# Order of the pieces within each visit to the halved array in an attention and feed-forward kernel

## The chip, the cores and the metric

The kernel runs on one core of a Trainium2 chip. The metric is the device time of one execution in microseconds. Three runs of the kernel before gave 1127.61, 1128.57 and 1129.76 us; the median is 1128.57 us.

## The reference

Two layers read the same input and a gate mixes them. The one is attention over four segments of 512 rows, with 32 heads of 20 columns; each segment also reads a memory that the earlier segments wrote. The other is a gated feed-forward layer, 640 wide with 1728 hidden columns. Cut to what matters here:

```python
for s in range(N):                       # N = 4 segments, L = 512 rows, 32 heads, Dh = 20
    logits = einsum("bhqd,bhkd->bhqk", qs, ks) * scale + mask
    p = softmax(logits, axis=-1)
    a_dot = einsum("bhqk,bhkd->bhqd", p, vs)
    a_mem = num / den                    # read of the memory of the earlier segments
    o = g * a_mem + (1.0 - g) * a_dot
    M = M + einsum("bhld,bhle->bhde", pk, vs)
...
b = (silu(x @ w1) * (x @ w3)) @ w2
return sigmoid(x . gate_w) * (o @ wo) + (1 - sigmoid(x . gate_w)) * b
```

The mask takes -1e9 for keys with an index above that of the query, so of the four blocks of 128 keys a block of 128 queries needs only those up to its own: 128, 256, 384 or 512 keys.

## The kernel before, in words

TensorE works on the projections and the feed-forward layer with the whole array (the shape `128*128` in the profile): 15 matmuls of 512 columns into one bank for a block of q, k, g or u (line 261), or a chain of matmuls of 320 columns for v (L372), f (L523) and op (L765). Between them stands the attention, whose contraction is only 60 or 62 rows. Two heads are laid one above the other, head 0 at partitions 0 and up, head 1 at 64 and up, and each head's matmul uses one half of the array's rows (`60*128` and `62*128`). Here a stretch of such matmuls is called a visit to the halved array, and the two matmuls of the two heads a piece.

For each pair of heads there are two kinds of unit:

- `s_unit(p, x)`, lines 560 to 580: the logits with queries in the partitions, from which VectorE takes each row's maximum (line 578, tile `m`). `x` = 0 holds the query blocks 0 and 1, pieces of 128 and 256 columns in one bank for each head; `x` = 1 a piece of 384; `x` = 2 a piece of 512.
- `t_unit(p, x)`, lines 596 to 613: the logits again, turned, with the row maxima as two more rows of the contraction (62 in place of 60), which ScalarE takes through exp into the tile `P` (line 609) and GpSimd masks (line 612). `x` = 0 is a piece of 512, `x` = 1 one of 384, `x` = 2 holds key blocks 3 and 2, pieces of 128 and 256 columns.

So a unit holds two banks, one for each head, and a unit with `x` = 0 of s or `x` = 2 of t holds two pieces in each. The banks come from `bank_tile` (line 120), which hands out eight in turn and takes the oldest free one; a bank is given again when the reader of its former tile is done.

Two pairs of heads make a quad (32 quads). `attention()` (line 712) runs through 40 slots for a quad; at slots 5, 15, 25 and 35 stands a visit, and in slot 5 `pv_quad` (line 617, tile `o`) comes ahead of it, on an array cut into four column strips (`128*32`). In each quad `m`, s units of quad `m` and t units of quad `m - 1` are issued; the table `VISITS` (line 709) says which: `(i, x)` is the pair of the quad and the unit. Between the visits a main loop hands out matmuls of the projections and the feed-forward layer by a credit in time. TensorE's order is that of the program; the order of the other engines is chosen by a scheduler when the kernel is built.

After the s units of a quad, `max_rows` (line 582) splits and turns the maxima and DMAs on GpSimd's queue put them into the two extra rows of `qk` (`qk<-mr`, line 594), for which the t units wait.

Of the kernel before, what the change touches and what calls it, by code (L numbers as in the profile page):

```python
# [17 lines left out]
P = 128  # L18
# [19 lines left out]
def gated_mix(ctx: ExitStack, tc: tile.TileContext, xT, wqk, wv, w13, w2, w2h, wo, beta, out):  # L38
# [81 lines left out]
    def bank_tile(name, hold=None):  # L120


        k = free.pop(0)
        ps = pp.tile([P, L], F32, tag=f"b{k}", name=name, bufs=1)
        if hold:
            held[k] = -hold
        else:
            free.append(k)
        return ps
# [410 lines left out]
    def load_pair(p):  # L540

        j = 2 * p
        c, h = divmod(j, H)
        t = qk[p % NST]
        for mb in {DH * h // P, (DH * h + 2 * DH - 1) // P}:
            assert ("q", c, mb) in stored and ("k", c, mb) in stored
        assert ("v", c, 3) in stored
        for i in range(2):
            here(nc.gpsimd.dma_start(t[64 * i:64 * i + RH], qkd[c][RH * (h + i):RH * (h + i + 1)]))  # L549
        if h % 8 == 0:  # L550
            bank["v"] = v = vg[j // 8 % NVG]
            here(nc.sync.dma_start(v[:, :, :VG], vd[c][:, :, VE * h:VE * h + VG]))
        if p % 2 == 0:
            bank["m"] = sp.tile([P, 16], F32, tag="m", name=f"m{j}", bufs=2)
        for i in range(2):
            o = VE * (h % 8 + i)
            heads[j + i] = dict(c=c, h=h + i, v=bank["v"][:, :, o:o + 32])
        pairs[p] = dict(t=t, m=bank["m"])

    def s_unit(p, t):  # L560

        u = pairs[p]
        m = u["m"]
        ps = [bank_tile(f"s{p}_{t}_{i}") for i in range(2)]
        for qb in ((0, 1), (2,), (3,))[t]:
            n = P * (qb + 1)
            o = 256 if qb == 1 else 0
            for i in range(2):
                q, k = (u["t"][64 * i:64 * i + RH, w] for w in range(2))
                nc.tensor.matmul(ps[i][:, o:o + n], q[:, qb * P:(qb + 1) * P], k[:, :n],  # L570
                                 start=qb != 1, stop=qb != 0, skip_group_check=True)
        for i in range(2):
            for qb in ((0, 1), (2,), (3,))[t]:
                n = P * (qb + 1)
                o = 256 if qb == 1 else 0
                junk = sp.tile([P, L], BF, tag="junk", name="junk", bufs=1)
                a = 8 * (p % 2) + 4 * i + qb
                nc.vector.tensor_tensor_reduce(out=junk[:, :n], in0=ps[i][:, o:o + n], in1=mask[:, L - n:],  # L578
                                               scale=1.0, scalar=-3.0e38, op0=ALU.add, op1=ALU.max,
                                               accum_out=m[:, a:a + 1])  # L580
# [15 lines left out]
    def t_unit(p, t):  # L596

        u = pairs[p]
        if t == 0:
            u["P"] = sp.tile([P, 2, 1280], F32, tag="P32", name=f"P{p}", bufs=NP)  # L600
        ps = [bank_tile(f"t{p}_{t}_{i}") for i in range(2)]
        for kb, q0, o in (((0, 0, 0),), ((1, P, 0),), ((3, 384, P), (2, 256, 256)))[t]:
            for i in range(2):
                q, k = (u["t"][64 * i:64 * i + RH + 2, w] for w in range(2))
                nc.tensor.matmul(ps[i][:, o:o + L - q0], k[:, kb * P:(kb + 1) * P], q[:, q0:],  # L605
                                 start=kb != 2, stop=kb != 3, skip_group_check=True)
        o, b, n = ((0, 0, 512), (512, 0, 384), (896, P, 384))[t]
        for i in range(2):
            last["exp"] = nc.scalar.activation(u["P"][:, i, o:o + n], ps[i][:, b:b + n], AF.Exp, scale=SCALE)  # L609
        for a, n in (((0, 1),), (), ((512, 1), (896, 2)))[t]:  # L610
            d = u["P"][:, :, a:a + n * P].rearrange("p h (a b) -> p h a b", b=P)
            nc.gpsimd.affine_select(d, d, pattern=[[0, 2], [0, n], [1, P]], base=0, channel_multiplier=-1,  # L612
                                    compare_op=ALU.is_ge, fill=0.0)
# [3 lines left out]
    def pv_quad(p):  # L617

        ps = bank_tile(f"o{p}")
        for kb, (o, n) in enumerate(PSEG):  # L620
            for i in range(4):
                nc.tensor.matmul(ps[32 * i:32 * i + 32, kb * P:], heads[2 * p + i]["v"][:, kb],  # L622
                                 pairs[p + i // 2]["P"][:, i % 2, o:o + n],
                                 start=kb == 0, stop=kb == 3, skip_group_check=True)
        ot = sp.tile([P, L], F32, tag="oq", name=f"oq{p}", bufs=1)
        nc.scalar.copy(ot, ps)
        c, h = heads[2 * p]["c"], heads[2 * p]["h"]
        nc.scalar.dma_start(od[c][h:h + 4].rearrange("h e n -> (h e) n"), ot)
        q = p // 2 % 8
        for b in OUT.get(q, ()):  # L630
            after(8, o_load, c, b)
        if q == 7:
            after(6 if c < NSEG - 1 else 2, o_sums, c)
# [63 lines left out]
    def after(n, f, *a):  # L697
        soon.append([n, f, a])

    def tick():  # L700
        for e in list(soon):
            e[0] -= 1
            if e[0] <= 0:
                soon.remove(e)
                e[1](*e[2])

    NQUAD = NJ // 4

    VISITS = {5: (((0, 0), (0, 1)), ((0, 0),)), 15: (((0, 2), (1, 0)), ((0, 1),)),
              25: (((1, 1), (1, 2)), ((0, 2),)), 35: ((), ((1, 0), (1, 1), (1, 2)))}  # L710

    def attention():


        for m in range(-1, NQUAD + 2):
            for n in range(40):
                if m == -1 and n < 40 - LEAD:
                    continue
                if n in VISITS:
                    us, ut = VISITS[n]  # L720
                    yield "visit"
                    if n == 5 and 0 <= m - 2 < NQUAD:
                        pv_quad(2 * m - 4)
                    if 0 <= m < NQUAD:
                        for i, x in us:
                            s_unit(2 * m + i, x)
                    if 0 <= m - 1 < NQUAD:
                        for i, x in ut:
                            t_unit(2 * m - 2 + i, x)
                    if n == 25 and 0 <= m < NQUAD:  # L730
                        after(6, max_rows, 2 * m)
                elif n in ((22, 32) if m < 0 else (27, 37)) and m + 1 < NQUAD:
                    load_pair(2 * (m + 1) + (n > 27))
                tick()
                yield m
# [160 lines left out]
    for n, (_, g) in enumerate(head):  # L896
# [7 lines left out]
        elif n == 9:  # L904
            gates()
    stores(True)
    att = attention()

    def begin():
# [101 lines left out]
```

## Time and profile before

| | |
|---|---|
| median of the three runs | 1128.57 us |
| profiled execution | 1128.27 us |
| its span in the profile | 1126.6 us (1.67 us lie around it) |
| PE, matmuls | 1118.2 us busy, 99% of the span |
| DVE, ACT, POOL | 51%, 43%, 48% busy |
| granted TensorE clock | 0.999 |

PE is TensorE's matmuls, PEld its weight loads, DVE VectorE, ACT ScalarE, POOL GpSimd, SP the queue of SyncE. In a timeline row stand the start in us, the length in us, the engine, the line, the operation, the tile written and the tiles read, the shape of the array, the operand's size and the count; rows of one kind that follow each other are merged, and the length of a merged row runs from its first start to its last end. A matmul's end in the profile is modelled and overlaps the next one, so the argument goes by starts. A window that ends between two instructions shows the start of each.

### The profile page before, as it was taken

The page shows a single profiled execution, that of the slowest core. Times are in us where ns is not written, and L with a number is a line of the kernel's source. Part 1 is how long each engine was busy: PE and PEld are TensorE (multiplying, and loading weights), DVE is VectorE, ACT ScalarE, POOL GpSimd, SP SyncE. Part 2 cuts the span into 40 slices and gives each one's busy share as a digit, 9 for nine tenths or more (in the row PEclk, how much of TensorE's full clock was granted, in tenths as well). Part 3 has the DMA queues.
Part 4 walks back from the last instruction along what each step waited for, and adds up shares of the span by engine and source line. Part 5 has one row for each costly group of instructions (what it writes and reads, how often), then busy time and mean ns, then how long its engine had stood idle before and what let it go on. Part 6 is the DMA issues. An engine that isn't in the chain of part 4 may idle for free.

```text
span 1126.6 us, 19474 instructions
## 1 busy us (share of the span) xinstructions
PE 1118.2 (99%) x6953; PEld 902.7 (80%) x6953; DVE 572.2 (51%) x1718; ACT 483.6 (43%) x988; POOL 544.2 (48%) x731
## 2 busy tenths in 40 slices
PE   9999999999999999999999999999999999999998
PEld 6988777877877888888977776788768778877888
DVE  5032564345555553565243667774546665651544
ACT  6255244544343242255355644535543444344040
POOL 5053356455455453454255346645764555465140
PEclk9999999999999999999999999999999999999999
DMA  9265753334243324535377874455654333342122
GB/s 328 80 235 204 235 135 94 96 81 114 79 112 103 97 65 121 140 86 177 109 244 246 269 213 133 103 133 167 165 130 106 86 100 95 100 136 76 49 59 94
DMA packets 85809, 152.01 MB, mean 135 GB/s; under 512 B 19920, under 2 KB 32720, under 8 KB 85712
## 3 DMA queue, kind: packets, MB, share of 16 engines
q1 hardware_dynamic: 55920, 95.01, 26.8%
q0 software_dynamic: 22880, 41.86, 15.5%
q10 hardware_dynamic: 6912, 13.90, 3.3%
q8 instruction: 55, 0.90, 0.3%
q14 instruction: 42, 0.34, 0.1%
HBM read 95.25 MB, written 54.53 MB: 133 GB/s over the span
## 4 chain that ended last, share of the span: by engine, by line
PE 93%; issue 2%; DVE 2%; DMA 1%; POOL 1%; ACT 0%; SPq 0%; POOLq 0%; DVEq 0%
PE g L261 17%; PE f L523 17%; PE u L261 16%; PE v L372 6%; PE k L261 6%; PE q L261 6%; PE o L622 6%; PE s L570 5%; PE op L765 4%; PE t L605 4%; PE pm L426 1%; PE nd L339 1%; DVE junk L578 1%; DMA qk<-mr 1%; PE pkt L411 1%
## 5 line engine op out<-in xcount | busy, mean ns | idle before, releaser
L578 DVE CUSTOM_DVE_ANT_0 junk<-s,mask 128x128 bf16<-128x128 f32 (+3 forms) x512 | 251.1, 490 | 190.5 <-PE s L570 151.3
L116 POOL TENSOR_TENSOR W<-wr,W 128x640 fp32r<-128x640 f32 (+1 forms) x126 | 197.6, 1572 | 204.2 <-ACT W L115 161.5
L609 ACT ACTIVATE P<-t 128x384 f32<-128x384 f32 (+1 forms) x384 | 174.5, 533 | 163.6 <-PE t L605 160.8
L261 PE MATMUL g<-X,W 128*128 128x512 f32 x840 | 216.3, 401 | 0.0
L612 POOL TENSOR_SCALAR_AFFINE_SELECT P<-P 128x256 f32<-128x256 f32 (+1 forms) x192 | 94.2, 497 | 235.0 <-ACT P L609 233.6
L523 PE MATMUL f<-W,ht 128*128 128x320 f32 x1312 | 204.7, 313 | 0.7 <-ACT acc L529 0.5
L261 PE MATMUL u<-X,W 128*128 128x512 f32 x780 | 201.0, 401 | 0.0
L523 PEld LDWEIGHTS f<-W,ht 128*128 128x128 f32 x1312 | 194.6, 189 | 7.2 <-issue 3.2
L261 PEld LDWEIGHTS g<-X,W 128*128 128x128 f32 x840 | 153.6, 188 | 39.8 <-issue 5.7
L261 PEld LDWEIGHTS u<-X,W 128*128 128x128 f32 x780 | 143.1, 188 | 36.2 <-issue 3.9
L115 ACT CAST W<-wr 128x640 fp32r<-128x640 f32 (+1 forms) x133 | 95.5, 730 | 74.7 <-PE u L261 23.1
L594 POOL DMA_DIRECT2D qk<-mr x128 | 73.5, 576 | 49.0 <-DVE mr L589 40.0
L531 DVE SCALAR_TENSOR_TENSOR acc<-f,cgate,acc 128x320 f32<-128x320 f32 x128 | 69.4, 547 | 40.4 <-PE f L523 39.7
L116 POOL TENSOR_TENSOR ht<-ft,ht 128x512 fp32r<-128x512 f32 x52 | 67.2, 1292 | 46.1 <-ACT ht L115 45.9
L261 PE MATMUL k<-X,W 128*128 128x512 f32 x300 | 77.1, 403 | 0.0
L261 PE MATMUL q<-X,W 128*128 128x512 f32 x300 | 75.4, 402 | 0.7 <-DVE X L116 0.6
L622 PE MATMUL o<-P,vg 128*32 128x512 f32 (+3 forms) x1024 | 75.7, 436 | 0.0
L765 PE MATMUL op<-W,oT 128*128 128x320 f32 x480 | 75.3, 313 | 0.0
L765 PEld LDWEIGHTS op<-W,oT 128*128 128x128 f32 x480 | 71.2, 189 | 2.5 <-issue 1.6
L372 PE MATMUL v<-W,X 128*128 128x320 f32 (+1 forms) x480 | 72.1, 311 | 0.5 <-DVE m L578 0.5
L372 PEld LDWEIGHTS v<-W,X 128*128 128x128 f32 x480 | 71.0, 189 | 1.4 <-DVE m L578 0.9
L549 POOL DMA_DIRECT2D qk<-qkd x128 | 70.1, 552 | 0.0
(106 smaller groups left out, 1087.0 us busy)
## 6 DMA issues: line engine op xcount, KB each, us to landing
qk<-qkd POOLq DMA_DIRECT2D x128, 240.0 KB, 3.9
wr<-in_w_dram SPq DMA_DIRECT2D x80, 320.0 KB
qkd<-qs SPq DMA_DIRECT2D x20, 512.0 KB
qkd<-ks SPq DMA_DIRECT2D x20, 512.0 KB
od<-oq ACTq DMA_DIRECT2D x32, 256.0 KB
wr<-in_wo_dram SPq DMA_DIRECT2D x20, 320.0 KB
vg<-vd SPq DMA_DIRECT2D x16, 336.0 KB
xr<-in_xT_dram SPq DMA_DIRECT2D x20, 256.0 KB
```

The costliest lines, as they stand in the source:

```text
L115: pin(nc.scalar.copy(dst[:, 0], src))
L116: (lo or nc.gpsimd.tensor_sub)(dst[:, 1], src, dst[:, 0].bitcast(F32))
L261: nc.tensor.matmul(ps, w[:, a, kb * P:(kb + 1) * P], x[:, b, kb, :], start=n == 0, stop=n == 14)
L372: nc.tensor.matmul(ps[:, :n1 - n0], x[:, a, kb, lb * P:(lb + 1) * P], wvt[kb][:, b, n0:n1], start=n == 0, stop=n == 14)
L523: nc.tensor.matmul(ps[:, :320], a, b, start=n == 0, stop=n == len(ms) - 1)
L549: here(nc.gpsimd.dma_start(t[64 * i:64 * i + RH], qkd[c][RH * (h + i):RH * (h + i + 1)]))
L578: nc.vector.tensor_tensor_reduce(out=junk[:, :n], in0=ps[i][:, o:o + n], in1=mask[:, L - n:], scale=1.0, scalar=-3.0e38, op0=ALU.add, op1= ...
L594: after(4 + 9 * k, lambda d=dst, r=r: here(nc.gpsimd.dma_start(d, mr[r:r + 8])))
L609: last["exp"] = nc.scalar.activation(u["P"][:, i, o:o + n], ps[i][:, b:b + n], AF.Exp, scale=SCALE)
L612: nc.gpsimd.affine_select(d, d, pattern=[[0, 2], [0, n], [1, P]], base=0, channel_multiplier=-1, compare_op=ALU.is_ge, fill=0.0)
L622: nc.tensor.matmul(ps[32 * i:32 * i + 32, kb * P:], heads[2 * p + i]["v"][:, kb], pairs[p + i // 2]["P"][:, i % 2, o:o + n], start=kb == 0 ...
L765: nc.tensor.matmul(ps[:, :320], oT[0][:, qb % 2, a, kb * P:(kb + 1) * P], ws[kb][:, b, 320 * hf:320 * hf + 320], start=n == 0, stop=n == 14)
```

## The change

Three things change, all of them order.

Within `s_unit` with `x` = 0, the piece of 256 columns is issued before that of 128 (it was the other way round), and the accumulation flags are exchanged with it; VectorE reads them in that order too. Within `t_unit` with `x` = 2, likewise 256 before 128. And the table `VISITS` now lists s and t units in one sequence, so that a t unit stands between two s units in slot 5 (`s01`, `t00`, `s00`) and slot 15 (`s02`, `t01`, `s10`). Slots 25 and 35 keep the order of their units. In the quad `m` = 1 the list is sorted, which gives the old order of units there.

```diff
     def s_unit(p, t):
...
-        for qb in ((0, 1), (2,), (3,))[t]:
+        for qb in ((1, 0), (2,), (3,))[t]:
             n = P * (qb + 1)
             o = 256 if qb == 1 else 0
             for i in range(2):
                 q, k = (u["t"][64 * i:64 * i + RH, w] for w in range(2))
                 nc.tensor.matmul(ps[i][:, o:o + n], q[:, qb * P:(qb + 1) * P], k[:, :n],
-                                 start=qb != 1, stop=qb != 0, skip_group_check=True)
+                                 start=qb != 0, stop=qb != 1, skip_group_check=True)
         for i in range(2):
-            for qb in ((0, 1), (2,), (3,))[t]:
+            for qb in ((1, 0), (2,), (3,))[t]:
...
     def t_unit(p, t):
...
-        for kb, q0, o in (((0, 0, 0),), ((1, P, 0),), ((3, 384, P), (2, 256, 256)))[t]:
+        for kb, q0, o in (((0, 0, 0),), ((1, P, 0),), ((2, 256, 256), (3, 384, P)))[t]:
             for i in range(2):
                 q, k = (u["t"][64 * i:64 * i + RH + 2, w] for w in range(2))
                 nc.tensor.matmul(ps[i][:, o:o + L - q0], k[:, kb * P:(kb + 1) * P], q[:, q0:],
-                                 start=kb != 2, stop=kb != 3, skip_group_check=True)
+                                 start=kb != 3, stop=kb != 2, skip_group_check=True)
...
-    VISITS = {5: (((0, 0), (0, 1)), ((0, 0),)), 15: (((0, 2), (1, 0)), ((0, 1),)),
-              25: (((1, 1), (1, 2)), ((0, 2),)), 35: ((), ((1, 0), (1, 1), (1, 2)))}
+
+    VISITS = {5: ("s01", "t00", "s00"), 15: ("s02", "t01", "s10"), 25: ("s11", "s12", "t02"), 35: ("t10", "t11", "t12")}
...
                 if n in VISITS:
-                    us, ut = VISITS[n]
                     yield "visit"
                     if n == 5 and 0 <= m - 2 < NQUAD:
                         pv_quad(2 * m - 4)
-                    if 0 <= m < NQUAD:
-                        for i, x in us:
-                            s_unit(2 * m + i, x)
-                    if 0 <= m - 1 < NQUAD:
-                        for i, x in ut:
-                            t_unit(2 * m - 2 + i, x)
+                    for kind, i, x in VISITS[n] if m != 1 else sorted(VISITS[n]):
+                        if kind == "s" and 0 <= m < NQUAD:
+                            s_unit(2 * m + int(i), int(x))
+                        elif kind == "t" and 0 <= m - 1 < NQUAD:
+                            t_unit(2 * m - 2 + int(i), int(x))
```

On PE, this is the visit of slot 15 in quad 3 before, with the feed-forward tile `f` that it interrupts; the last two numbers of a row are the array's output partitions and the piece's columns.

```order
L523 MATMUL f_0_0_1_2114<-W_1509,ht_1_1663 128x320 x2
L570 MATMUL s_2_0_2120<-qk_88 128x512
L570 MATMUL s_2_1_2121<-qk_88 128x512
L570 MATMUL s_0_0_2128<-qk_89 128x128
L570 MATMUL s_0_1_2129<-qk_89 128x128
L570 MATMUL s_0_0_2128<-qk_89 128x256
L570 MATMUL s_0_1_2129<-qk_89 128x256
L605 MATMUL t_1_0_2142<-qk_86 128x384
L605 MATMUL t_1_1_2143<-qk_86 128x384
L523 MATMUL f_0_0_1_2114<-W_1509,ht_1_1663 128x320
```

The same place in the changed kernel:

```order
L523 MATMUL f_0_0_1_2114<-W_1509,ht_1_1663 128x320 x2
L570 MATMUL s_2_0_2120<-qk_88 128x512
L570 MATMUL s_2_1_2121<-qk_88 128x512
L605 MATMUL t_1_0_2128<-qk_86 128x384
L605 MATMUL t_1_1_2129<-qk_86 128x384
L570 MATMUL s_0_0_2134<-qk_89 128x256
L570 MATMUL s_0_1_2135<-qk_89 128x256
L570 MATMUL s_0_0_2134<-qk_89 128x128
L570 MATMUL s_0_1_2135<-qk_89 128x128
L523 MATMUL f_0_0_1_2114<-W_1509,ht_1_1663 128x320
```

The piece of 384 moved from the end to the second place, and that of 128 from the second place to the end, behind the 256 of its own unit. What stands around the visit is the same.

Still on PE, the next visit (slot 25), as a piece of the difference: the units keep their places and the two pieces of the t unit change theirs.

```order
 L570 MATMUL s_2_0_2189<-qk_89 128x512
 L570 MATMUL s_2_1_2190<-qk_89 128x512
+L605 MATMUL t_2_0_2197<-qk_86 128x256
+L605 MATMUL t_2_1_2198<-qk_86 128x256
 L605 MATMUL t_2_0_2197<-qk_86 128x128
 L605 MATMUL t_2_1_2198<-qk_86 128x128
-L605 MATMUL t_2_0_2197<-qk_86 128x256
-L605 MATMUL t_2_1_2198<-qk_86 128x256
 L523 MATMUL f_0_2_0_2175<-W_1509,ht_1_1663 128x320
```

Here too the visit now ends with 128 columns.

On ACT, at the visit of slot 5 in quad 3, where the output of `pv_quad` (`o`) is copied to `oq` and stored to `od`, and the unit `t00` goes through exp into `P`:

```order
 L626 COPY oq_2042<-o_2025 128x512
+L609 ACTIVATE P_2053<-t_0_0_2054 128x512
 L628 DMA od_76<-oq_2042 128x512
-L609 ACTIVATE P_2067<-t_0_0_2068 128x512
-L609 ACTIVATE P_2067<-t_0_1_2069 128x512
+L609 ACTIVATE P_2053<-t_0_1_2055 128x512
 L529 ACTIVATE acc_1928<-f_0_2_1_2019,cgate 128x320
```

The first head's exp now stands ahead of the DMA that stores `oq`; apart from the numbers in the names the rest is as it was.

## The prediction

> **What bounds the kernel now.** I read the page first: the engines' shares, the granted clock, the chain that ended last.
>
> ```profile
> span 1126.6 us, 19474 instructions
> PE 1118.2 (99%) x6953; PEld 902.7 (80%) x6953; DVE 572.2 (51%) x1718; ACT 483.6 (43%) x988; POOL 544.2 (48%) x731
> PEclk9999999999999999999999999999999999999999
> PE 93%; issue 2%; DVE 2%; DMA 1%; POOL 1%; ACT 0%; SPq 0%; POOLq 0%; DVEq 0%
> ```
>
> TensorE's queue sets the time: 93% of the chain is matmuls, the clock is granted in full, and no other engine is above 51%. So what the change saves in TensorE's queue arrives at the end nearly whole, and what it moves on the other engines costs only where TensorE waits for it. "Busy" says little here, since the matmuls' ends are modelled; I go by the distance from start to start. Two runs of plain matmuls give the rate (timeline, one of u and one of f; below them the page's groups, with the mean of one):
>
> ```profile
> 499.93 1.99 PE L261 MATMUL u<-X,W 128*128 128x512 f32 x8
> 510.02 1.34 PE L523 MATMUL f<-W,ht 128*128 128x320 f32 x8
> ...
> L261 PE MATMUL u<-X,W 128*128 128x512 f32 x780 | 201.0, 401 | 0.0
> L523 PE MATMUL f<-W,ht 128*128 128x320 f32 x1312 | 204.7, 313 | 0.7 <-ACT acc L529 0.5
> ```
>
> A single one lasts 0.40 and 0.31 us, so seven steps take 1.59 and 1.03: 0.227 us for 512 columns and 0.147 for 320, or 0.44 to 0.46 ns a column. At that rate a piece of 128 columns streams in 0.06 us, 256 in 0.12, 384 in 0.17 and 512 in 0.23.
>
> Next the timeline in narrow windows, at the two visits whose order the section on the change shows. Slot 15, before:
>
> ```profile
> 204.23 0.30 PEld L570 LDWEIGHTS s<-qk 60*128 60x128 f32 x4 [0.20 <-issue]
> 204.58 0.19 PEld L570 LDWEIGHTS s<-qk 60*128 60x128 f32 x2
> 204.63 0.33 PE L570 MATMUL s<-qk 60*128 60x256 f32 x2
> 204.68 0.19 PEld L605 LDWEIGHTS t<-qk 62*128 62x128 f32 x2
> 204.81 0.34 PE L605 MATMUL t<-qk 62*128 62x384 f32 x2
> 205.07 0.19 PEld L523 LDWEIGHTS f<-W,ht 128*128 128x128 f32 x1 [0.20 <-issue]
> ```
>
> The four loads of the first row are those of the pieces 512 and 128. Alone a pair of loads spans 0.19 and four span 0.30, so the second pair starts 0.11 after the first: a load takes 0.11 us, and only one piece's load runs ahead. The load for the 256 waits until 204.58, when the 128 begins to stream (204.23 + 0.11 + 0.23, rounded); the 128 is through at 204.63, where the profile puts the 256's start, but its load is there only at 204.69. The next load (204.68) and the 384's start, 0.18 after the 256's where it streams in 0.12, show the hole: 0.06 here. A piece of 128 with another piece behind it thus costs a load, 0.11, not its 0.06. After the last piece the next load, for the whole array, comes only when the 384 is through: 204.81 + 0.17 = 204.98, load at 205.07, 0.09 later. Nothing is loaded ahead across that border.
>
> Slot 25, the next visit:
>
> ```profile
> 209.27 0.30 PEld L570 LDWEIGHTS s<-qk 60*128 60x128 f32 x4 [0.20 <-issue]
> 209.55 0.39 PE L570 MATMUL s<-qk 60*128 60x512 f32 x2
> 209.78 0.22 PE L605 MATMUL t<-qk 62*128 62x128 f32 x2
> 209.79 0.19 PEld L605 LDWEIGHTS t<-qk 62*128 62x128 f32 x2
> 209.84 0.33 PE L605 MATMUL t<-qk 62*128 62x256 f32 x2
> 210.10 0.19 PEld L523 LDWEIGHTS f<-W,ht 128*128 128x128 f32 x1
> ```
>
> The 256's load starts at 209.79 with the 128, so it can stream only from 209.90, 0.05 to 0.06 after 209.84; 209.90 + 0.12 + 0.08 = 210.10.
>
> Slot 5, the visit before these two, with `o` ahead of it:
>
> ```profile
> 196.02 0.61 PE L622 MATMUL o<-P,vg 128*32 128x512 f32 x4
> 196.44 0.51 PE L622 MATMUL o<-P,vg 128*32 128x384 f32 x4
> 197.63 0.29 PE L622 MATMUL o<-P,vg 128*32 128x128 f32 x4
> 197.85 0.30 PEld L570 LDWEIGHTS s<-qk 60*128 60x128 f32 x4 [0.20 <-issue]
> 198.36 0.39 PE L605 MATMUL t<-qk 62*128 62x512 f32 x2
> 198.68 0.19 PEld L523 LDWEIGHTS f<-W,ht 128*128 128x128 f32 x1 [0.30 <-issue]
> ```
>
> From first load to the load after the last piece the three visits take 0.83, 0.84 and 0.83 us, each with one 128 that has a piece behind it. The gap at the end is the same 0.08 to 0.09, whatever the last piece (198.36 + 0.23 = 198.59 for the 512).
>
> **The change part by part.** *The 128 goes last.* The same four pieces then need 0.11 for the first load, 0.17 + 0.23 + 0.12 + 0.06 of streaming with every later load covered (0.11 under 0.17, 0.23 and 0.12), and 0.09 at the end: 0.78 in any order of the first two. Against 0.83 that is 0.05 a visit, the 0.11 less 0.06. How many visits:
>
> ```profile
> L570 PE MATMUL s<-qk 60*128 60x128 f32 x128 | 17.9, 272 | 0.0
> L605 PE MATMUL t<-qk 62*128 62x128 f32 x128 | 16.6, 229 | 0.2
> ```
>
> 256 matmuls, two to a piece, are 128 pieces, one to a visit. In quad 1 the sorted list keeps the old order of units, and the 128 of `s00` and `s10` still has a unit behind it: 126 visits gain. 126 x 0.05 = 6.3 us.
>
> *The end of a visit after 128 columns* is not in the trace for these shapes. The nearest row is `o`, which ends with 128: its 512 takes 0.42 (196.02 to 196.44), so its 128 takes 0.11; four start at 197.63, close behind each other, and are through 0.11 to 0.13 later, at 197.74 to 197.76; the next load starts at 197.85, 0.09 to 0.11 later. I take 0.09, as at the other three ends. Bounds: 0.11, if the short piece leaves 0.02 more to wait for, and 0.08; that is 0.03 to 0.06 a visit, 3.8 to 7.6 us.
>
> [...]
>
> *The units change places* (slots 5 and 15). Whether TensorE waits for a bank hangs on when its reader is done. The waits of now (list of waits, PE and PEld):
>
> ```profile
> PE t L605 <- DMA qk<-mr: 0.3, 1, 0.3
> PE t L605 <- DVE m L578: 0.2, 1, 0.2
> PEld s L570 <- DVE m L578: 1.0, 4, 0.4
> PEld t L605 <- DVE m L578: 0.4, 1, 0.4
> ```
>
> All waits for the maxima's reads come to 1.6 us. In slots 5 and 15 the last banks of a visit now go to VectorE, not ScalarE; VectorE reads the same tiles in the same total time, and its last tile sits two banks later in the turn than before, so it is asked for later. I take 0, with 1 us either way. `t00` and `t01` start 0.23 earlier (0.11 + 0.12 no longer ahead of them), so ScalarE and GpSimd get them earlier; against the rows of `qk<-mr` this costs 0.23 only where it was late already, one visit: nothing.
>
> *Within a unit*, VectorE reads 256 ahead of 128: same instructions, nothing. *The DMA `od<-oq`* now stands behind one exp on ACT, which itself waits for `t00`: about 0.6 us later.
>
> ```profile
> L609 ACT ACTIVATE P<-t 128x512 f32<-128x512 f32 x128 | 69.6, 596 | 66.0 <-PE t L605 63.3 <-POOL W L116 2.1 <-POOL ht L116 0.5
> ```
>
> It is read again at the earliest six slots on, and a quad of 40 slots lasts some 25 us (next slot-5 visit at 223.11, below), so 3.8 us hide it. If that cover were gone, it would cost 0.6 at four segment ends, 2.4 us. On SP and POOL's queue nothing is passed.
>
> ```profile
> 223.11 0.41 PEld L570 LDWEIGHTS s<-qk 60*128 60x128 f32 x6 [0.20 <-issue]
> ```
>
> The sum: 1128.27 (the profiled execution, 0.30 under the median) - 6.3 = 1122.0 us; a span of 1120.3.
>
> **The rivals.** *No gain.* If loads ran further ahead, the load behind a 128 would be hidden anyway, and order inside a visit would not matter: 126 x 0 and 1128.3 us. The same follows if the wait at the border grew by 0.05 after a short piece. Against the first: in all three visits the second load comes 0.11 after the first though nothing streams yet, and the third only as the second piece begins. Against the second: 0.08 to 0.09 at all four ends shown. [...] Chance 0.05 for the hidden loads and 0.04 for the longer border, 0.09 together.
>
> *Slower: the s unit at the end of slots 5 and 15.* Its two banks are freed by VectorE after all of the visit's s pieces. If the matmuls behind the visit or the next visit ask for them first, TensorE waits at the border, as it does here:
>
> ```profile
> 719.29 0.19 PEld L605 LDWEIGHTS t<-qk 62*128 62x128 f32 x2 [0.42 <-DVE m L578]
> ```
>
> A wait of 0.42 in a third of the 62 visits is 8.8 us, and 1128.3 - 6.3 + 8.8 = 1130.8 us. It undoes the gain from 0.10 us a visit on average (6.3 / 62) and makes the kernel measurably slower from 0.14. For it: VectorE is late around 719. Against it: 1.6 us of such waits in all, where the last s tile was asked for two banks sooner. Chance 0.04.
>
> *Absorbed.* The time returns at waits of TensorE that don't move with it, such as weight loads. The chain has 7% outside PE; if five times that share were lost, 35% of 6.3, 1124.2 us remain. This lies within the range.
>
> **How the numbers follow.** A change of 0.2%, 2.26 us, is about what a measurement of this kernel can tell from none. The forecast, with its absorbed form and the smaller price, has 0.87; no gain 0.09; slower 0.04. The low end: 7.6 us for 126 visits and 1 us of waits gone, 1119.7. The high end: 3.8 us less 1 us of new waits gives 1125.5; it reaches a little into no gain, 1126.0. Faster by over 0.2% (under 1126.3) 0.87, same 0.09, slower 0.04.
>
> **What would show it.** Right: in the changed profile a visit of four pieces takes 0.78 from its first load to the load of the whole array, in all four slots but quad 1; the load of the piece behind the 256 starts with the 256; after the 128 the gap is 0.09; the span is near 1120.3; waits for `m` stay under 3 us. Wrong: visits still at 0.83 (no gain, by a longer gap at the end or by loads that were hidden), or visits at 0.78 with new idle rows before PEld, released by `junk` or `m` of L578, right behind slots 5 and 15.

## The result, and the profile after

The changed kernel takes 1121.9 us (median of six runs, 1120.77 to 1122.51) where the kernel before takes 1128.25 us (six runs, the three above and three more); the ratio is 0.9944, with a 95% interval of 0.9933 to 0.9954. The profiled execution took 1122.51 us, 5.8 less than that of before, and is the slowest of the six. One of the four executions of the experiment e3 below took 3762.61 us, for a reason that was not followed; its median of 1134.01 us includes it, and the other three took 1133.88 to 1134.09 us.

The page after, the same rows as before:

```profile
span 1120.8 us, 19482 instructions
PE 1112.7 (99%) x6953; PEld 909.5 (81%) x6953; DVE 571.4 (51%) x1718; ACT 483.1 (43%) x988; POOL 542.7 (48%) x731
PEclk9999999999999999999999999999999999999999
PE 90%; issue 4%; DMA 2%; DVE 1%; POOL 1%; ACT 1%; SPq 0%; POOLq 0%; DVEq 0%
```

The granted clock is 1.000 (0.999 before), the engines' counts are the same and the work of DVE, ACT and POOL is the same to within 1.5 us; the matmuls' busy time and the span fell by about the same, 5.5 and 5.8 us. The loads' busy time (PEld) rose by 6.8 us and the chain's share outside PE from 7 to 10%, though the kernel is faster, so neither row prices the change.

The visit of slot 15 in quad 3, in narrow windows of the timeline:

```profile
204.54 0.19 PEld L570 LDWEIGHTS s<-qk 60*128 60x128 f32 x2 [0.20 <-ACT acc L529]
204.65 0.19 PEld L605 LDWEIGHTS t<-qk 62*128 62x128 f32 x2
204.88 0.37 PEld L570 LDWEIGHTS s<-qk 60*128 60x128 f32 x4
205.06 0.28 PE L570 MATMUL s<-qk 60*128 60x256 f32 x2
205.18 0.22 PE L570 MATMUL s<-qk 60*128 60x128 f32 x2
205.33 0.19 PEld L523 LDWEIGHTS f<-W,ht 128*128 128x128 f32 x1
```

From 204.54 to 205.33 it takes 0.79 us; before it took 0.84. The load of the last piece starts with the 256 at 205.06 (four loads from 204.88 span 0.37, where two span 0.19: the second pair starts 0.18 later). The 256 streams until 205.18, longer than the 0.11 of that load, so the 128 starts at once. It is through at 205.24, and the next load comes at 205.33, 0.09 later.

Slot 25, the next visit: its first load, the load of the 128 with the start of the 256, and the load behind the visit:

```profile
209.54 0.19 PEld L570 LDWEIGHTS s<-qk 60*128 60x128 f32 x2 [0.20 <-ACT acc L529]
210.06 0.19 PEld L605 LDWEIGHTS t<-qk 62*128 62x128 f32 x2
210.06 0.34 PE L605 MATMUL t<-qk 62*128 62x256 f32 x4
210.33 0.19 PEld L523 LDWEIGHTS f<-W,ht 128*128 128x128 f32 x1
```

0.79 us again, where 0.83 stood before. Slot 5, the visit ahead of these two:

```profile
198.19 0.19 PEld L570 LDWEIGHTS s<-qk 60*128 60x128 f32 x2 [0.20 <-issue]
198.71 0.28 PE L570 MATMUL s<-qk 60*128 60x256 f32 x2
198.98 0.19 PEld L523 LDWEIGHTS f<-W,ht 128*128 128x128 f32 x1
```

0.79 too. Over all visits of a slot in the two traces, the median from the first load's start to the start of the first load behind the visit (worked out from the traces, like the other medians by slot below) falls from 831 to 790 ns (slot 5, 31 and 30 visits), 840 to 790 (slot 15), 836 to 786 (slot 25) and 839 to 793 (slot 35): 41, 50, 50 and 46 ns. With 30, 30, 31 and 32 visits that is 5.75 us, with the three visits of the first and last quads 5.9.

### The profile page after: what moved, and what is told of

It is laid out like the page before. It is cut to its first block, busy times and chain, and to the rows that moved or that the text cites. A ratio compares the mean times of both kernels' runs of the same rounds, so it can differ in the third digit from the quotient of the medians.

```text
span 1120.8 us, 19482 instructions
## 1 busy us (share of the span) xinstructions
PE 1112.7 (99%) x6953; PEld 909.5 (81%) x6953; DVE 571.4 (51%) x1718; ACT 483.1 (43%) x988; POOL 542.7 (48%) x731
## 4 chain that ended last, share of the span: by engine, by line
PE 90%; issue 4%; DMA 2%; DVE 1%; POOL 1%; ACT 1%; SPq 0%; POOLq 0%; DVEq 0%
PE f L523 18%; PE g L261 17%; PE u L261 16%; PE q L261 6%; PE o L622 6%; PE k L261 5%; PE s L570 5%; PE op L763 4%; PE v L372 4%; PE t L605 4%; PE pm L426 1%; PE nd L339 1%; POOL W L116 1%; DMA wr<-in_wqk_dram 1%; DVE junk L578 1%
## 5 line engine op out<-in xcount | busy, mean ns | idle before, releaser
L578 DVE CUSTOM_DVE_ANT_0 junk<-s,mask 128x256 bf16<-128x256 f32 (+3 forms) x512 | 250.9, 490 | 188.8 <-PE s L570 148.9
L570 PE MATMUL s<-qk 60*128 60x128 f32 (+3 forms) x512 | 73.8, 346 | 0.0
```

## The experiments

The theory: one load runs ahead, and takes 0.11 us (204.54 to 204.65 above); a piece of 128 columns streams in 0.06 (209.78 to 209.84 before), so with a piece behind it in the visit it costs the 0.11, and only as the last piece its own 0.06. The rivals: the units' order brings the change through banks and readers; loads are hidden anyway; the s unit at the end of a visit makes TensorE wait.

**e1, the pieces alone.** The kernel before, with the order inside the units as changed (the accumulation flags and VectorE's reads with it) and the old table of visits:

```diff
-        for qb in ((0, 1), (2,), (3,))[t]:
+        for qb in ((1, 0), (2,), (3,))[t]:
...
-        for kb, q0, o in (((0, 0, 0),), ((1, P, 0),), ((3, 384, P), (2, 256, 256)))[t]:
+        for kb, q0, o in (((0, 0, 0),), ((1, P, 0),), ((2, 256, 256), (3, 384, P)))[t]:
```

> Only the pieces inside a unit change places (256 before 128); the units keep the old order. Theory (a 128 with a piece behind it costs a load of 0.11 us, and costs its 0.06 only as the last piece): slots 25 and 35 gain, 64 visits at about 0.05, slots 5 and 15 keep 0.83 to 0.84 a visit, since a unit of 384 or 512 still follows: 3.1 us, 1125.1 us. Rival A (the gain comes from the units' order, by banks or by the readers' order): 1128.3 us. Rival B (256 ahead of 128 is worth the gain by itself, wherever it stands): 1121.9 us.

Measured: 1124.87 us against 1128.56 for the kernel before, a ratio of 0.9969 (0.9958 to 0.9979): 3.7 us less, where 3.1 were expected. First and last load of a visit of slot 5 (198.66, 199.49) and of slot 25 (210.04, 210.82):

```profile
198.66 0.19 PEld L570 LDWEIGHTS s<-qk 60*128 60x128 f32 x2 [0.20 <-issue]
199.49 0.19 PEld L523 LDWEIGHTS f<-W,ht 128*128 128x128 f32 x1 [0.30 <-issue]
210.04 0.19 PEld L570 LDWEIGHTS s<-qk 60*128 60x128 f32 x2 [0.20 <-issue]
210.82 0.19 PEld L523 LDWEIGHTS f<-W,ht 128*128 128x128 f32 x1
```

Slot 5, where the 128 has moved behind its 256 but 384 and 512 still follow, takes 0.83 as before; slot 25, where it has become the last, 0.78. The medians of slots 5 and 15 are 839 and 832 ns (831 and 840 before), those of slots 25 and 35 786 and 792. So it isn't the order of 256 and 128 that counts, but whether something follows. Rival B falls.

**e2, the units alone.** The changed kernel with 128 ahead of 256 again:

```diff
-        for qb in ((1, 0), (2,), (3,))[t]:
+        for qb in ((0, 1), (2,), (3,))[t]:
...
-        for kb, q0, o in (((0, 0, 0),), ((1, P, 0),), ((2, 256, 256), (3, 384, P)))[t]:
+        for kb, q0, o in (((0, 0, 0),), ((1, P, 0),), ((3, 384, P), (2, 256, 256)))[t]:
```

> Only the units change places; inside a unit the 128 stays ahead of the 256. Theory: every 128 still has a piece behind it, so no visit gets shorter: 1128.3 us, within 1 us. Rival A (units' order): 1121.9 us, or 1125 for a half of it. The rival of the prediction on the other side (the s unit at the end of slots 5 and 15 makes TensorE wait for VectorE) would show alone here: over 1129.5 us, with longer waits for m.

Measured: 1127.53 us against 1128.56, ratio 0.999 (0.9981 to 0.9999): 1.0 us less, at the edge of what can be told from nothing. The visit of slot 15, with the starts of the 128 and the 256 and the load behind:

```profile
205.51 0.19 PEld L570 LDWEIGHTS s<-qk 60*128 60x128 f32 x2 [0.20 <-ACT acc L529]
206.03 0.23 PE L570 MATMUL s<-qk 60*128 60x128 f32 x2
206.09 0.33 PE L570 MATMUL s<-qk 60*128 60x256 f32 x2
206.35 0.19 PEld L523 LDWEIGHTS f<-W,ht 128*128 128x128 f32 x1
```

0.84 as before (medians 841 and 844 ns in slots 5 and 15): the units' order alone shortens no usual visit, and rival A falls. Nor does the s unit at the end of slots 5 and 15 show a cost. In this trace the time that visits take over their slot's median comes to 2.6 us, and to 4.6 before; the longest case of slot 15 before (1.58 us at 718.1, with the wait of 0.42 for `m` that the prediction showed) is gone. That would account for the 1.0, but one trace on each side doesn't show it.

**e5, the other half.** The changed kernel with only the t unit put back, so that slots 5 and 15 stay as changed:

```diff
-        for kb, q0, o in (((0, 0, 0),), ((1, P, 0),), ((2, 256, 256), (3, 384, P)))[t]:
+        for kb, q0, o in (((0, 0, 0),), ((1, P, 0),), ((3, 384, P), (2, 256, 256)))[t]:
```

> The changed kernel with the two pieces of the t unit (slots 25 and 35) put back to 128 before 256; slots 5 and 15 as changed. Theory: the two halves of the change add up. Slots 5 and 15 gain 60 visits x 0.047 = 2.8 us, and the units' order gives the 1.0 us that it gave alone: 1128.3 - 3.8 = 1124.5 us; visits of slots 25 and 35 back at 0.83 to 0.84, of 5 and 15 at 0.79. Rival (the units' order was worth nothing, 1.0 was scatter): 1125.5 us. Rival (it needs all four slots): over 1127 us.

Measured: 1123.94 us against 1128.61, ratio 0.9958 (0.9945 to 0.997): 4.7 us less, where 3.8 were expected; the interval reaches from 3.4 to 6.2. First load and load behind, slots 15 and 25:

```profile
204.17 0.19 PEld L570 LDWEIGHTS s<-qk 60*128 60x128 f32 x2 [0.20 <-ACT acc L529]
204.96 0.19 PEld L523 LDWEIGHTS f<-W,ht 128*128 128x128 f32 x1
209.15 0.19 PEld L570 LDWEIGHTS s<-qk 60*128 60x128 f32 x2 [0.20 <-ACT acc L529]
209.99 0.19 PEld L523 LDWEIGHTS f<-W,ht 128*128 128x128 f32 x1
```

0.79 where the 128 is last, 0.84 where it is not. The halves e1 and e5 come to 8.4 us together, the whole change to 6.35. By visits they should come to 7.0 (65 and 62 visits at 0.047, and the 1.0 of the units' order; the 64 and 60 of the expectations leave out visits of the first quad, one of which gains in both halves); the intervals of 2 to 3 us cover that difference, so I make nothing of it.

**e3, the suspected cost doubled.** The changed kernel, with each 256 cut into two matmuls of 128 columns; for the s unit:

```diff
-        for qb in ((1, 0), (2,), (3,))[t]:
-            n = P * (qb + 1)
-            o = 256 if qb == 1 else 0
+        for qb, k0, n in (((1, 0, P), (1, P, P), (0, 0, P)), ((2, 0, 384),), ((3, 0, L),))[t]:
+            o = (256 if qb == 1 else 0) + k0
```

> The changed kernel with each piece of 256 cut into two of 128 (the same columns, the same sums): visits end 128, 128, 128, two of them with a piece behind. Theory: a covered 256 (0.117) becomes two loads (0.107 to 0.11 each), 0.10 more for each of 128 visits: 12.8 us over the changed kernel, 1134.7 us, visits of 0.89. [...] If loads were hidden: 1121.9 us.

Measured: 1134.01 us, ratio 1.0051 to the kernel before (1.0036 to 1.0066), and 12.1 us over the changed kernel where 12.8 were expected. The visit of slot 15:

```profile
205.31 0.19 PEld L569 LDWEIGHTS s<-qk 60*128 60x128 f32 x2 [0.20 <-ACT acc L529]
205.83 0.30 PEld L569 LDWEIGHTS s<-qk 60*128 60x128 f32 x4
205.94 0.19 PEld L569 LDWEIGHTS s<-qk 60*128 60x128 f32 x2
206.00 0.28 PE L569 MATMUL s<-qk 60*128 60x128 f32 x2
206.20 0.19 PEld L523 LDWEIGHTS f<-W,ht 128*128 128x128 f32 x1
```

With three pieces of 128 the loads stand at 205.83 and 205.94: 0.11 apart although each piece streams in 0.06. The visit takes 0.89, 0.10 more. That is the price of the prediction by itself: 12.1 us over 128 visits are 0.095 each, two loads of 0.11 in place of 0.12. Had the loads been hidden, the time would have stayed at 1121.9. The loads do run ahead, but only by one piece: that of the second 128 comes at 205.83, when the first 128 starts, and that of the third 0.11 later, at 205.94.

**e4, fewer borders.** If a border costs its 0.09 and a load of 0.11 on either side, fewer and longer visits should pay. The changed kernel with three visits of four units in a quad (`max_rows` and the loads of the next pairs are moved to fit):

```diff
-    VISITS = {5: ("s01", "t00", "s00"), 15: ("s02", "t01", "s10"), 25: ("s11", "s12", "t02"), 35: ("t10", "t11", "t12")}
+    VISITS = {5: ("s01", "t00", "s02", "s00"), 18: ("s11", "t01", "s12", "s10"), 31: ("t02", "t10", "t11", "t12")}
```

> The changed kernel with the twelve units of a quad in three visits of four units in place of four visits of three (loads of the next pairs moved behind the last visit). Theory (the border costs: 0.09 and a load of 0.11 at each end): 32 visits fewer at 0.40 each, 12.8 us, and one 128 a quad has a piece behind it again, 1.6 us: 1110.7 us. Rival (banks): a visit now takes all eight banks, so its last unit or the tile behind it waits for readers in the same visit; 0.2 us on average at 96 visits would make it 1130 us.

Measured: 1170.23 us, ratio 1.0372 (1.0351 to 1.0394). The rival was right in kind, and its 0.2 a visit was far too small. The visit of slot 5 at 228.3, and four of the longest waits of the visits' loads in the list of waits:

```profile
228.33 0.19 PEld L570 LDWEIGHTS s<-qk 60*128 60x128 f32 x2 [0.20 <-issue]
229.11 0.18 PEld L570 LDWEIGHTS s<-qk 60*128 60x128 f32 x1 [0.30 <-ACT oq L626]
229.43 0.19 PEld L570 LDWEIGHTS s<-qk 60*128 60x128 f32 x2
229.43 0.44 PE L570 MATMUL s<-qk 60*128 60x256 f32 x2
229.80 0.19 PEld L261 LDWEIGHTS u<-X,W 128*128 128x128 f32 x1
...
PEld s L570 <- DVE m L578: 12.5, 27, 0.8
PEld s L570 <- ACT oq L626: 6.9, 23, 0.3
PEld t L605 <- ACT P L609: 6.8, 25, 0.4
PEld s L570 <- DMA qk<-qkd: 4.5, 6, 1.7
```

This visit takes 1.47 us where its five pieces need about 1.02 (0.79 and 0.23 for one more of 512, all later loads covered). The seventh and eighth banks of the visit are not free in time: the first head's load of the 256 waits until 229.11 for ScalarE, the second head's until 229.43, and only then do the second head's 256 and the 128 of both heads follow, with the next load at 229.80. Nor is it a rare visit: the medians are 1.47 us in slots 5 and 18 and 1.40 in slot 31, and all visits together take 150.3 us where those of the changed kernel take 105.9. Waiting shown in these four rows is 30.7 us in all, 26.2 of it in the three rows for banks. So here the wait for banks, not the border, limits how long a visit may be. What the loads of the pairs, moved behind the last visit, add to it (`qk<-qkd`, 4.5 us in the list) was not told apart.

**e6, the maxima earlier.** Visits of slot 35 take 2.4 us over their median in the changed kernel, nearly all in eight of them, and the list of waits puts 0.9 us of that on the bank of `max_rows`. The changed kernel with

```diff
-                        after(6, max_rows, 2 * m)
+                        after(4, max_rows, 2 * m)
```

> The changed kernel with max_rows called 4 slots behind slot 25 in place of 6, so that the bank of its split is read earlier. Of the time that visits of slot 35 take over their median, 2.4 us in the changed kernel, most is spent waiting for that bank (released by VectorE's subtraction of line 141). Theory (the wait is for the bank's reader): up to 2 us less, 1120.0 us. Rival (the reader is late because the maxima are late, so the call's place changes nothing, or ScalarE is held up by its wait): 1121.9 us or more.

Measured: 1124.46 us, ratio 0.9958 (0.9945 to 0.9971). That is 2.5 us over the 1121.9 of the changed kernel, but the two were not measured side by side and the intervals of their ratios overlap, so a loss is not shown, only that there is no gain. The visits of slot 35 still take 2.3 us over their median, and the same list still shows 0.9 us for that bank. The theory fell: the bank's reader comes no earlier. In the visit of slot 35 at 240.2, for example, VectorE's subtraction (line 141) starts at 240.61 in the changed kernel and at 240.66 in e6, 0.42 us behind the visit's first load in both, and right behind an instruction on the tile `fu` (line 492). What orders them so was not followed. None of the kernels tried beats the changed one.

## Why the prediction was right

*The sum.* Forecast 1122.0, measured 1121.9 (profiled 1122.51, span 1120.8 where 1120.3 stood). The term that carried it, 126 visits at 0.05, measured 41 to 50 ns by slot, 0.047 on average, 5.9 us in place of 6.3. That the medians differ by 6.35, so close to the 6.3, is in part luck: the term was 0.4 too large, and the units' order, taken as 0, gave 1.0 alone in e2, so the one may have made up for the other. e1, e2 and e5 show that it takes both parts of the change in slots 5 and 15 and the pieces alone in 25 and 35, as the working had it; e3 shows the price itself. No run shows the smaller price a visit that the 0.87 also counts: the visits became 41 to 50 ns shorter, and the loads in e3 stand 0.11 us apart.

*The end of the visit after 128 columns*, for which there was no row, was taken as 0.09 from `o`; the visits after show 0.09 (205.24 to 205.33). Slot 5 gained least, 41 ns: it had ended with 512 columns, after which the gap was a few ns shorter, and the rounding of the rows to 0.01 us had hidden that. By the medians the next load starts 318 ns after the 512 in slot 5 and 269 after the 384 in slot 15; less the some 232 and 176 that such pieces take from start to start in slot 25, an estimate of the gap is 86 ns against 93.

*The units' places*: taken as 0 with 1 us either way. e2 gives 1.0 us less, at the edge of its interval. The fear of the rival on the other side did not come true in the changed kernel: the waits of PEld for `m` fell from 2.3 to 1.3 us. (The prediction's 1.6 us for such waits left out a `v` tile's, 0.9 on PEld and 0.5 on PE, and a third of 62 visits at 0.42 is 8.7, not 8.8; neither moves the forecast.) But the wait for the rows of the maxima grew in the profiled run:

```profile
PEld s L570 <- DVE m L578: 0.5, 2, 0.4
PEld t L605 <- DMA qk<-mr: 0.7, 1, 0.7
PE t L605 <- DMA qk<-mr: 0.4, 1, 0.4
```

It is one visit, at 818.1, 1.90 us long where 0.79 is usual; `t00`, now second in its visit, waited there until 819.40:

```profile
812.91 1.14 POOL L594 DMA_DIRECT2D qk<-mr  x2 [1.71 <-DVE mr L589]
818.56 0.18 PEld L570 LDWEIGHTS s<-qk 60*128 60x128 f32 x1 [0.24 <-DMA qk<-qkd]
819.40 0.22 PEld L605 LDWEIGHTS t<-qk 62*128 62x128 f32 x2 [0.65 <-DMA qk<-mr]
```

The same slot and quad waited for nothing in the trace of before. There the two DMAs were issued at 817.89, 5.27 us ahead of their visit, and here 5.23 ahead; but the longest of the four `qk<-mr` DMAs around the visit took 4.5 us from issue to landing there and 6.1 here (the rows of before, and below them the landings in the changed kernel):

```profile
817.89 1.14 POOL L594 DMA_DIRECT2D qk<-mr  x2 [1.71 <-DVE mr L589]
DMA to landing us min/median/max: 2.0/3.3/4.5
...
DMA to landing us min/median/max: 2.2/4.2/6.1
```

Of the 1.1 us that the visit is too long, 0.42 lies at the second head's load of the s unit (818.14 to 818.56), which waits for another DMA, and the rest at `t00`. The earlier place of `t00` accounts for at most 0.23 of it, as the prediction priced it; late transfers in that run account for the rest. e2 and e5 have the same order of units, and no visit of slots 5 and 15 in their traces takes over 1.05 us. The step "one visit: nothing" was still too quick in that which visit is late changes from run to run. Why the transfers were late was not followed.

*The DMA of `oq`*: six slots is not the least, as line 633 reads `od` again after two in the last segment. No t unit stands behind that last `pv_quad`, so nothing hung on it.

*Absorbed.* All 131 visits together took 6.4 us less (112.3 to 105.9; 5.9 by the medians, the rest by fewer or shorter waits), the span 5.8: what PE's queue saved came through but for 0.6, and that in the slowest of six runs. Which rows took the 0.6 was not followed.

## What to carry to other kernels

Where loads run one ahead, as in these traces, a matmul whose columns stream faster than a load (0.06 us against 0.11 here) costs the load, unless nothing of its own kind follows: look for the start of the next load in narrow windows of the timeline, and put the shortest piece where the queue stops anyway: here that was ahead of the change of the array's shape, where the next load came 0.09 us after the last piece was through. Price it by start-to-start distances, since the busy row of PE stays at 99% before and after. And before making such stretches longer to save borders, count the banks: in e4, the one case tried, stretches that needed all eight cost more than the borders they saved (150.3 us for all visits against 105.9).

## What the runs showed that was not expected

In the four visits below a late bank cost more than the time by which it was late. The visit of slot 35 at 240.15 in the kernel before, with VectorE's read that frees the second head's bank of the t unit:

```profile
240.53 0.16 DVE L141 TENSOR_TENSOR ns<-m,nh 128x16 fp32r<-128x16 f32 x1
...
240.49 0.18 PEld L605 LDWEIGHTS t<-qk 62*128 62x128 f32 x1
240.66 0.46 PE L605 MATMUL t<-qk 62*128 62x128 f32 x3
240.74 0.29 PEld L605 LDWEIGHTS t<-qk 62*128 62x128 f32 x3
241.16 0.19 PEld L261 LDWEIGHTS u<-X,W 128*128 128x128 f32 x1
```

The first head's load for the 128 ran ahead at 240.49 and its matmul started at 240.66; the second head's load waited until 240.74, when the read was over. That is 0.08 behind the start of the first head's matmul, but the visit took from 240.15 to 241.16, 1.01 us or 0.18 over the usual. My reading is that the wait stands at the load, so that this load did not run ahead of the stream, and its 0.11 came on top of the 0.08. Three more visits of slot 35 before, at 315.54, 684.74 and 816.17, show the like: with loads late by 0.11, 0.20 and 0.09 they take 0.21, 0.30 and 0.19 more than the median, 0.10 over the lateness each time.
